# Turning the far half of the normalised input on VectorE, from an exchanged copy kept in DRAM, instead of on TensorE

## The chip, the cores and the metric

The kernel runs on one core of one Trainium2 chip. The metric is the device time of one execution in microseconds (us); of three runs of the kernel before, the median is 1872.5 us (1872.37 to 1872.6).

## The reference

One transformer block in float32, for 2048 positions of 1024 features and 32 heads of 32. The part that the change touches is the input of the first projections, the normalised x.

```python
qkv = layernorm(x) @ wqkv                       # 2048 x 1024 by 1024 x 3072
pq, pk = q_h @ w_phi_h, k_h @ w_phi_h           # per head, 32 x 32
phi = concat(softmax(p), softmax(-p))           # for q and for k
o = phi_q (phi_k^T v) / (phi_q . sum phi_k + 1e-6)
h = x + o @ wo
out = h + relu(layernorm(h) @ w1) @ w2          # 1024 -> 3584 -> 1024
```

## The kernel before, in words

Every large product is made of matmuls with 128 x 128 stationary and 128 x 512 moving values. Float32 precision is kept by splitting each operand into a high part (float32 rounded to the matmul's type) and a low part (what is left); `mm3` (lines 182 to 184) adds high by high, high by low and low by high, so three matmuls make one **step** of the work.

The first stretch of the program, the projections, has 96 **items** of eight steps: 768 steps, counted from 0. An item multiplies one tile of 128 positions of normalised x by 512 columns of weights, one step for each of eight blocks k of 128 features. Eight items in a row (eight tiles) share the same eight weight tiles and make a **group** of 64 steps. The order is: for the near half of the positions (tiles 0 to 7), four groups for keys and values, kv (steps 0 to 255), and two for queries, q (256 to 383); then the same for the far half, tiles 8 to 15 (steps 384 to 767).

The names that matter around the change:

- `Units` hands out weights. A raw weight tile comes by DMA from SyncE's queue (SP) into one of six `raw` buffers; ScalarE (ACT) makes the high part (line 125), and VectorE (DVE) or GpSimd (POOL) the low part (line 129) into one of ten `w` buffers. Eight of the ten belong to the group in work, so only two weights of the next group, k0 and k1, can be made early. The others, k2 to k7, are made in the few steps around a **group change** (steps 64, 128, 192, 256, 320, 384, 448 and so on), each as soon as the last item of the old group has released a buffer. On POOL stand the lows of k2, k4 and k6 for kv groups, and of k3, k4, k6 and k7 for the near q groups.
- A tile of x is loaded, `ln_stats` (DVE) and `ln_power` (POOL, three small instructions, lines 231 to 233) give its mean and scale, `ln_norm` (ACT, line 239) normalises it, and `ln_turn` turns it: eight 128 x 128 transposes by TensorE (PE, line 246) into two banks of PSUM, from which `split` writes high (ACT, line 178) and low part (DVE, line 179) into the tile's `xT`. For the far tiles the statistics are taken early (x is loaded, read and let go), the normalising and turning happen beside the second q group, one tile in eight steps from step 321, and x is loaded a second time for it.
- `kv_z` (POOL, lines 452 and 454) adds each item's features of the keys into `zacc`. `q_fourth` (POOL, line 544) multiplies two small tiles per q item.
- The two last matrices are multiplied by a scheme with seven products in place of eight, which needs sums of blocks of w1 and w2. `t_load` (SP, line 353) brings a piece b of 512 KB, `t_sum` (POOL, line 363) makes four sums of 128 x 256 in it, `t_store` (SP, line 366) puts it back in DRAM. The table `sums_at` sets the step of each of the 56 pieces, and `home` its buffers: two in `tsp`, two in `fp` while that pool lives (until step 256), later two in `fp_ln`, the pool of the normalised tiles `xn`.

Nothing is scheduled at run time. `when(step, f, ...)` and `do(item, k, f, ...)` put calls into a table, and the program is written out in that order; each engine then runs its own instructions strictly in order, waiting for data and buffers. An instruction that waits holds up all that stand behind it on its engine. This holds for SP's DMA issues as well.

## Time and profile before

| | us |
|---|---|
| median of 3 runs | 1872.5 |
| the profiled execution, by its own clock outside | 1870.48 |
| its span, from first to last instruction | 1868.7 |
| PE busy in the span | 1856.5 |
| DVE busy | 1063.8 |
| ACT busy | 770.5 |
| POOL busy | 979.0 |

The profile is of one execution. A line such as "start, length, engine, line of the program, operation, out<-in, shapes, count, [idle before <- who ended the wait]" is one instruction, or several equal ones in a row. The table of waits gives for each waiting engine and line the time in total, the times, and the longest. Durations of neighbouring instructions on an engine can overlap a little, since they are pipelined: the distance of the starts is the cost.

### The profile page before, as it was taken

The numbers are of one execution on the slowest core, as the hardware profiler recorded it, in microseconds if no ns is written. First come the engines' busy times: TensorE is split into PE (matmuls) and PEld (weight loads), VectorE is DVE, ScalarE is ACT, GpSimd is POOL, SyncE is SP. The second block draws the span as 40 slices with busy tenths as digits, with TensorE's granted clock in tenths as the row PEclk, the third lists the DMA queues.
The fourth block names the chain that finished last, engine by engine and source line by source line (L and its number), as shares of the span: only waits on it lengthen the run. The fifth ranks groups of instructions, "written<-read, shape, count | busy, mean of one in ns | idle before, by whom it ended". The sixth has DMA issues, their size and how long they took to land.

```text
span 1868.7 us, 28840 instructions
## 1 busy us (share of the span) xinstructions
PE 1856.5 (99%) x10064; PEld 1516.3 (81%) x10064; DVE 1063.8 (57%) x1655; ACT 770.5 (41%) x1379; POOL 979.0 (52%) x991
## 2 busy tenths in 40 slices
PE   9999999999999999999999999999999999999999
PEld 7777788888887777888888888888888888888887
DVE  7787678677689878575555653443433333343333
ACT  5322245233333333354455554444444444444442
POOL 4887745888947988343333222222344444444443
PEclk9999999999999999999999999999999999999999
DMA  7988798666575676887888975666677677777765
GB/s 229 286 294 288 231 289 270 190 203 202 178 227 181 223 243 203 280 278 232 247 262 259 324 249 184 193 201 205 225 223 215 216 218 239 238 215 217 216 216 177
DMA packets 333635, 433.04 MB, mean 232 GB/s; under 512 B 28720, under 2 KB 194608, under 8 KB 333488
## 3 DMA queue, kind: packets, MB, share of 16 engines
q1 hardware_dynamic: 299696, 414.41, 70.1%
q10 hardware_dynamic: 33792, 16.78, 3.2%
q8 instruction: 79, 1.29, 0.3%
q14 instruction: 68, 0.56, 0.1%
HBM read 293.21 MB, written 137.89 MB: 231 GB/s over the span
## 4 chain that ended last, share of the span: by engine, by line
PE 93%; DVE 3%; POOL 1%; issue 1%; ACT 0%; DMA 0%; SPq 0%; ACTq 0%; DVEq 0%; POOLq 0%
PE mm L182 24%; PE mm L183 24%; PE mm L184 24%; PE ac L182 4%; PE ac L184 4%; PE ac L183 4%; PE tp L184 2%; PE tp L183 2%; PE tp L182 2%; PE tp L246 1%; PE ac L465 1%; PE ac L650 1%; DVE qsm L534 0%; DVE qe L637 0%; POOL w L129 0%
## 5 line engine op out<-in xcount | busy, mean ns | idle before, releaser
L129 POOL TENSOR_TENSOR w<-raw,w 128x512 fp32r<-128x512 f32 x353 | 469.0, 1331 | 698.3 <-ACT w L125 663.2
L125 ACT ACTIVATE w<-raw 128x512 fp32r<-128x512 f32 x686 | 409.4, 626 | 508.8 <-PE mm L184 232.4
L129 DVE TENSOR_TENSOR w<-raw,w 128x512 fp32r<-128x512 f32 x333 | 271.0, 815 | 511.6 <-ACT w L125 507.6
L182 PE MATMUL mm<-w,xT 128*128 128x512 f32 x768 | 306.0, 398 | 0.0
L183 PE MATMUL mm<-w,xT 128*128 128x512 f32 x768 | 300.2, 391 | 0.4 <-POOL w L401 0.4
L184 PE MATMUL mm<-w,xT 128*128 128x512 f32 x768 | 299.6, 390 | 0.0
L182 PE MATMUL mm<-hT,w 128*128 128x512 f32 x672 | 261.5, 389 | 0.0
L183 PE MATMUL mm<-hT,w 128*128 128x512 f32 x672 | 261.5, 389 | 0.0
L184 PE MATMUL mm<-hT,w 128*128 128x512 f32 x672 | 261.5, 389 | 0.0
L182 PEld LDWEIGHTS mm<-w,xT 128*128 128x128 f32 x768 | 144.4, 188 | 35.2 <-issue 4.1
L184 PEld LDWEIGHTS mm<-w,xT 128*128 128x128 f32 x768 | 144.4, 188 | 30.9
L363 POOL TENSOR_TENSOR b<-b 128x256 f32<-128x256 f32 x176 | 143.6, 816 | 48.0 <-DMA b<-in_w_dram 38.6
L183 PEld LDWEIGHTS mm<-w,xT 128*128 128x128 f32 x768 | 144.6, 188 | 29.2 <-POOL w L401 1.0
L184 PE MATMUL mm<-w 128*128 128x512 f32 x392 | 152.6, 389 | 0.0
L182 PE MATMUL mm<-w 128*128 128x512 f32 x392 | 152.6, 389 | 0.0
L183 PE MATMUL mm<-w 128*128 128x512 f32 x392 | 152.6, 389 | 0.0
L182 PEld LDWEIGHTS mm<-hT,w 128*128 128x128 f32 x672 | 126.2, 188 | 26.4
L183 PEld LDWEIGHTS mm<-hT,w 128*128 128x128 f32 x672 | 126.2, 188 | 26.2
L184 PEld LDWEIGHTS mm<-hT,w 128*128 128x128 f32 x672 | 126.2, 188 | 26.0
L183 PEld LDWEIGHTS mm<-w 128*128 128x128 f32 x392 | 73.6, 188 | 15.3
L184 PEld LDWEIGHTS mm<-w 128*128 128x128 f32 x392 | 73.6, 188 | 15.2
L182 PEld LDWEIGHTS mm<-w 128*128 128x128 f32 x392 | 73.6, 188 | 15.3
(173 smaller groups left out, 3106.0 us busy)
## 6 DMA issues: line engine op xcount, KB each, us to landing
raw<-t SPq DMA_DIRECT2D x224, 256.0 KB, 3.9
raw<-ad SPq DMA_DIRECT2D x196, 256.0 KB, 3.0
raw<-in_w_dram SPq DMA_DIRECT2D x168, 256.0 KB, 3.1
ad<-c SPq DMA_DIRECT2D x112, 256.0 KB, 3.6
b<-in_w_dram SPq DMA_DIRECT2D x44, 512.0 KB, 5.8
t<-b SPq DMA_DIRECT2D x44, 512.0 KB, 5.0
ad<-s SPq DMA_DIRECT2D x84, 256.0 KB, 4.1
ed<-qe ACTq DMA_DIRECT2D x64, 256.0 KB, 4.1
```

The lines of the kernel that those rows point to most:

```text
L125: nc.scalar.activation(w[:, 0, :], raw[1], AF.Copy)
L129: eng.tensor_tensor(out=w[:, 1, :], in0=raw[1], in1=w[:, 0, :].bitcast(F32), op=ALU.subtract)
L182: pe.matmul(ps, a_hi, b_hi, start=first, stop=False, skip_group_check=more)
L183: pe.matmul(ps, a_hi, b_lo, start=False, stop=False, skip_group_check=more)
L184: pe.matmul(ps, a_lo, b_hi, start=False, stop=last, skip_group_check=more)
L246: pe.transpose(pt[:, k, :], xn[:, (4 * j + k) * P:(4 * j + k + 1) * P], ident)
L363: pool.tensor_tensor(out=tsum[*u, *out], in0=tsum[*u, *a], in1=tsum[*u, *b], op=ALU.subtract)
L465: pe.matmul(kv_ps[s][g][32 * i:32 * (i + 1), 0:64], vt[:, 32 * h:32 * (h + 1)], phi[:, 64 * h:64 * (h + 1)], start=first, stop=last)
L650: pe.matmul(banks[g][32 * c:32 * (c + 1), 256 * j:256 * (j + 1)], kvL[rows, 2 * q + h // 4, 32 * (h % 4):32 * (h % 4 + 1)], phT_of[u - 1 + ...
```

## The change

The far tiles are no longer turned by PE. Their early pass keeps its result: after `ln_power`, the new `far_norm` (ACT) normalises the tile and writes it with the blocks of 32 features in another order, and `far_keep` (SP) stores it in DRAM as `xm`, with 32-row blocks of positions and quarters of features exchanged. Later `far_back` (SP) loads that copy (four tiles at steps 250 to 265, the other four 32 steps before their turning), and `far_turn` (DVE) turns it in place by 32 x 32 blocks, which with the exchange makes the full transpose. `far_high` (ACT) and `far_low` (POOL, 128 x 1024) make the two parts of `xT`, reading the turned tile through `far_view`, in which neighbouring elements lie 256 apart. 

The early pass goes from one tile in 16 steps (from step 80) to one in 26. The turning goes from one tile in 8 steps (from 321) to one in 11 (from 330, so that the last four tiles are turned in the first items of the far half, at steps 374 to 417). In `sums_at` the two pieces at 332 and 342 are taken away and the ten from step 202 to 296 become twelve from step 198 to 293, seven to ten steps apart in place of nine to nineteen.

```diff
+    xm = {t: dram.tile([P, D], F32, name=f"xm{t}") for t in range(HT, NT)}
...
     def ln_load(key, parts):
-        xin[key] = xlp.tile([P, D], F32, name="xl") if key[0] == "x" and key[1] >= HT and key[1] % 4 > 1 else \
-            lnp.tile([P, D], F32, name="xin")
+        xin[key] = lnp.tile([P, D], F32, name="xin")
...
+    def far_norm(t):
+        sc, src = xst.pop(("s", t)), xin.pop(("s", t))
+        xin["m", t] = y = lnp.tile([P, D], F32, name="xin")
+        act.activation(y.rearrange("p (a c k) -> p c a k", a=4, c=NK), src.rearrange("p (c a k) -> p c a k", a=4, c=NK),
+                       AF.Identity, bias=sc[:, 1:2], scale=sc[:, 0:1])
+
+    def far_keep(t):
+        sp.dma_start(xm[t].rearrange("(a t) (g x) -> (t g) a x", a=4, g=4),
+                     xin.pop(("m", t)).rearrange("p (a x) -> p a x", a=4))
+
+    def far_back(t):
+        xnt["x", t] = y = xlp.tile([P, D], F32, name="xl") if t % 4 > 1 else fp_ln.tile([P, D], F32, name="xn")
+        sp.dma_start(y, xm[t])
+
+    def far_turn(t):
+        v.transpose(xnt["x", t], xnt["x", t])
+
+    def far_view(y):
+        return y.rearrange("p (g c t) -> p c t g", g=4, c=NK)
+
+    def far_high(t):
+        act.activation(xT[t][:, 0].rearrange("p c (t g) -> p c t g", g=4), far_view(xnt["x", t]), AF.Copy)
+
+    def far_low(t):
+        lo, hi = (xT[t][:, s].rearrange("p c (t g) -> p c t g", g=4) for s in (1, 0))
+        pool.tensor_tensor(out=lo, in0=far_view(xnt.pop(("x", t))), in1=f32(hi), op=ALU.subtract)
...
-            early = 80 + 16 * (t - HT)
+            early, late_ = 80 + 26 * (t - HT), 330 + 11 * (t - HT)
             when(early, ln_load, ("s", t), x_part(t))
-            when(early + 18, ln_stats, ("s", t))
-            when(early + 18, xin.pop, ("s", t))
-            when(early + 22, ln_power, ("s", t))
-            load_ = turn - 88 + 8 * (t - HT) if t < HT + 4 else turn - 36
-            stages = (load_, None, None, turn - 8, turn + 1, turn + 1)
+            when(early + 12, ln_stats, ("s", t))
+            when(early + 16, ln_power, ("s", t))
+            when(early + 20, far_norm, t)
+            when(early + 23, far_keep, t)
+            when(250 + 5 * (t - HT) if t < HT + 4 else late_ - 32, far_back, t)
+            do(n, 0, x_open, t)
+            for step, f in ((0, far_turn), (6, far_high), (10, far_low)):
+                when(late_ + step, f, t)
+            continue
...
-    sums_at = [30, 39, 47, 55] + [64 * i + k for i in (1, 2, 3) for k in sixth] + \
-        [266, 276, 286, 296, 332, 342, 352, 362, 372] + [64 * i + k for i in (6, 7, 8, 9) for k in sixth] + [650]
+    sums_at = [30, 39, 47, 55] + [64 * i + k for i in (1, 2) for k in sixth] + \
+        [198, 205, 212, 219, 226, 233, 243, 253, 263, 273, 283, 293, 352, 362, 372] + [64 * i + k for i in (6, 7, 8, 9) for k in sixth] + [650]
...
-        when(step - (7 if 256 < step < 400 else 15), t_load, w, p, j, home)
+        when(step - (7 if 240 < step < 400 else 15), t_load, w, p, j, home)
```

Three places of POOL's queue, each before and after the change. The line numbers of the changed kernel are higher by 27: 363 becomes 390 (sums), 454 becomes 481 (`kv_z`), 544 becomes 571 (`q_fourth`); 129 (lows of weights) and 231 to 233 (`ln_power`) keep theirs. In the names, w is a weight, raw its source, b or xn a piece of sums, zacc the sum over the keys' features, sc or scx the mean and scale of a tile of x, xT a turned tile.

The first place is the group change at step 128. Before, POOL's row from the `ln_power` at step 118 to the lows of k4 and k6:

```order
L231 TENSOR_SCALAR scx<-mv 128x1
L232 TENSOR_TENSOR scx<-scx,half 128x1
L233 TENSOR_SCALAR scx<-mv,scx 128x1
L363 TENSOR_TENSOR b<-b 128x256 x2
L129 TENSOR_TENSOR w<-raw,w 128x512
L363 TENSOR_TENSOR b<-b 128x256
L454 TENSOR_TENSOR zacc_361<-zacc_361,kphi 128x512
L363 TENSOR_TENSOR b<-b 128x256
L129 TENSOR_TENSOR w<-raw,w 128x512 x2
```

The same place on POOL in the changed kernel, where the first w is again k2 and the pair k4 and k6:

```order
L390 TENSOR_TENSOR b<-b 128x256 x2
L129 TENSOR_TENSOR w<-raw,w 128x512
L390 TENSOR_TENSOR b<-b 128x256
L231 TENSOR_SCALAR sc<-mv 128x1
L232 TENSOR_TENSOR sc<-sc,half 128x1
L233 TENSOR_SCALAR sc<-mv,sc 128x1
L481 TENSOR_TENSOR zacc_369<-zacc_369,kphi 128x512
L390 TENSOR_TENSOR b<-b 128x256
L129 TENSOR_TENSOR w<-raw,w 128x512 x2
```

The `ln_power` (now at step 122) has moved from ahead of the sums to a place behind k2 and ahead of k4 and k6.

The second place is the group change at step 256, the opening of the first q group. Before, POOL's lows are k3, and after one `kv_z` and one sum k4, k6 and k7 together:

```order
L363 TENSOR_TENSOR b<-b 128x256 x3
L129 TENSOR_TENSOR w<-raw,w 128x512
L454 TENSOR_TENSOR zacc_363<-zacc_363,kphi 128x512
L363 TENSOR_TENSOR b<-b 128x256
L129 TENSOR_TENSOR w<-raw,w 128x512 x3
L454 TENSOR_TENSOR zacc_363<-zacc_363,kphi 128x512
```

The same place on POOL in the changed kernel, from the four sums of the piece at step 243:

```order
L390 TENSOR_TENSOR b<-b 128x256 x4
L129 TENSOR_TENSOR w<-raw,w 128x512
L481 TENSOR_TENSOR zacc_371<-zacc_371,kphi 128x512
L129 TENSOR_TENSOR w<-raw,w 128x512
L231 TENSOR_SCALAR sc<-mv 128x1
L232 TENSOR_TENSOR sc<-sc,half 128x1
L233 TENSOR_SCALAR sc<-mv,sc 128x1
L129 TENSOR_TENSOR w<-raw,w 128x512
L390 TENSOR_TENSOR b<-b 128x256
L129 TENSOR_TENSOR w<-raw,w 128x512
L390 TENSOR_TENSOR b<-b 128x256 x3
L481 TENSOR_TENSOR zacc_371<-zacc_371,kphi 128x512
```

A whole piece (step 243) now ends just ahead of k3, an `ln_power` (step 252) stands between k4 and k6, and the first sum of the next piece (step 253) between k6 and k7.

The third place is the first group of the far half, steps 394 to 448, up to the row that is followed by the low of k2 for the group change at step 448. Before, from the second of its pieces:

```order
L363 TENSOR_TENSOR b<-b 128x256 x4
L454 TENSOR_TENSOR zacc_360<-zacc_360,kphi 128x512
L363 TENSOR_TENSOR xn<-xn 128x256 x4
L454 TENSOR_TENSOR zacc_360<-zacc_360,kphi 128x512
L363 TENSOR_TENSOR xn<-xn 128x256 x4
L454 TENSOR_TENSOR zacc_360<-zacc_360,kphi 128x512
L363 TENSOR_TENSOR b<-b 128x256 x4
L454 TENSOR_TENSOR zacc_360<-zacc_360,kphi 128x512
L363 TENSOR_TENSOR b<-b 128x256 x2
L129 TENSOR_TENSOR w<-raw,w 128x512
```

The same place on POOL in the changed kernel:

```order
L390 TENSOR_TENSOR b<-b 128x256 x3
L281 TENSOR_TENSOR xT<-xl,xT 128x1024
L390 TENSOR_TENSOR b<-b 128x256
L481 TENSOR_TENSOR zacc_368<-zacc_368,kphi 128x512
L390 TENSOR_TENSOR xn<-xn 128x256 x4
L281 TENSOR_TENSOR xT<-xl,xT 128x1024
L481 TENSOR_TENSOR zacc_368<-zacc_368,kphi 128x512
L390 TENSOR_TENSOR xn<-xn 128x256 x4
L481 TENSOR_TENSOR zacc_368<-zacc_368,kphi 128x512
L390 TENSOR_TENSOR b<-b 128x256 x4
L481 TENSOR_TENSOR zacc_368<-zacc_368,kphi 128x512
L390 TENSOR_TENSOR b<-b 128x256 x2
```

The low parts of tiles 14 and 15 (line 281) have come into this row; that of tile 13 stands one piece earlier, and that of tile 12 just behind the low of k6 for the group change at step 384.

4 lines of the change are left out of this document (2 added, 2 removed).

## The prediction, as it was put on record

> **What bounds the kernel now.** I read the page first, then the waits of PE, and then PE's own row of time where the far tiles are turned.
>
> ```profile
> span 1868.7 us, 28840 instructions
> PE 1856.5 (99%) x10064; PEld 1516.3 (81%) x10064; DVE 1063.8 (57%) x1655; ACT 770.5 (41%) x1379; POOL 979.0 (52%) x991
> PE 93%; DVE 3%; POOL 1%; issue 1%; ACT 0%; DMA 0%; SPq 0%; ACTq 0%; DVEq 0%; POOLq 0%
> ```
>
> PE works through 99% of the span, and the chain that ended last is PE for 93%. So the time falls by what PE no longer does, and rises by what PE has to wait that it doesn't wait now.
>
> ```profile
> PE ac L650 <- DVE qe L637: 2.8, 2, 2.4
> ```
>
> This is the first of five rows, the longest in total: no line of PE waits more than 2.8 us in the whole program, and none of the five lies in the stretch that changes. There is no wait to win there, only work.
>
> ```profile
> 268.78 0.39 PE L184 MATMUL mm<-w,xT 128*128 128x512 f32 x1
> 269.01 1.03 PE L246 MATMUL tp<-ident,xn 128*128 128x128 f32 x8
> 269.80 0.48 PE L182 MATMUL mm<-w,xT 128*128 128x512 f32 x1
> 270.12 0.40 PE L183 MATMUL mm<-w,xT 128*128 128x512 f32 x1
> ```
>
> A matmul comes every 0.227 us (0.68 us a step, 5.44 us an item). Between 269.01 and 270.12 stand eight transposes and one matmul: 1.11 - 0.23 = 0.88 us for the transposes.
>
> ```profile
> 269.17 0.87 PE tp L246 x8
> ...
> 313.61 0.87 PE tp L246 x8
> ```
>
> In the chain, the first and last of the eight far tiles lie 44.44 us apart, 6.35 us an item in place of 5.44: 0.91 us a tile.
>
> **The change part by part.** *PE's transposes.* 64 of 176 leave. Eight times 0.91 is **7.3 us less**, and this is the whole gain that the change can have.
>
> *What the turning costs elsewhere.*
>
> ```profile
> L637 DVE STREAM_TRANSPOSE qe<-qe 128x1024 f32<-128x1024 f32 x32 | 39.3, 1227 | 7.5 <-POOL qe L631 5.6 <-POOL qe L626 1.8
> L179 DVE TENSOR_TENSOR xT<-tp,xT 128x512 fp32r<-128x512 f32 x32 | 20.7, 679 | 11.1 <-ACT xT L178 11.1
> L631 POOL TENSOR_TENSOR qe<-qe,qden 128x1024 f32<-128x1024 f32 x26 | 50.3, 1935 | 3.1 <-DVE qden L621 3.0
> L129 POOL TENSOR_TENSOR w<-raw,w 128x512 fp32r<-128x512 f32 x353 | 469.0, 1331 | 698.3 <-ACT w L125 663.2 <-DMA ad<-s 12.1 <-DVE c L866 8.3
> L667 DVE TENSOR_TENSOR oT<-ac,oT 128x512 fp32r<-128x512 f32 x32 | 20.2, 673 | 3.3 <-ACT oT L657 3.3
> L781 DVE STREAM_TRANSPOSE y<-xin 128x1024 f32<-128x1024 f32 x4 | 8.2, 2040 | 1.2 <-ACT xin L796 1.2
> 262.00:311.00 49.00, 49.00 (x246) 41.12 (x245) 41.92 (x66) 28.05 (x38) 24.30 (x42) 1.00 0.90 276
> ```
>
> DVE gives up two differences of 0.68 us a tile (1.36) and gets one turn, for which the in-place turn of the same size is the row: 1.23. That is even. Beside the second q group DVE is busy 41.92 of 49 us, and there the items get 14% shorter, so its cover is thin: 41.92 over 7.7 items of 6.35 is 5.4 us of work for an item that will last 5.44. I cost it at nothing, because an item's bank is needed again only three items later; once DVE falls over 10 us behind, PE waits. ACT trades two copies of 512 for one of 1024 beside 28 of 49 us: nothing. A load, a store and a load in place of two loads are eight transfers of 512 KB more, on queues that wait for nothing of theirs: nothing by themselves.
>
> POOL gets `far_low`, **d** us each, eight times, and no row shows a POOL difference that reads elements 256 apart. Below, the shortest POOL row of that size (L631, one operand repeated) is 1.94. Contiguous, two lows of 512 take 2.66. Above, DVE pays 2.04 in place of 1.23 where its turn runs over spread elements (L781 against L637), a factor 1.66: 4.4 by that. The nearest row is the difference of the same kind, L129, so d = 2.66, with 1.94 and 4.4 kept.
>
> [...]
>
> *What gets in front of weights.* POOL matters to PE only at group changes, where it must make lows between the release of a buffer and the use. So each is a sum of its own.
>
> At step 128:
>
> ```profile
> 109.41 0.22 POOL L231 TENSOR_SCALAR scx<-mv 128x1 f32<-128x1 f32 x1 [2.91 <-DVE mv L224]
> ...
> 111.04 1.55 POOL L363 TENSOR_TENSOR b<-b 128x256 f32<-128x256 f32 x2
> 112.92 1.30 POOL L129 TENSOR_TENSOR w<-raw,w 128x512 fp32r<-128x512 f32 x1 [0.33 <-ACT w L125]
> ...
> 118.22 3.00 POOL L129 TENSOR_TENSOR w<-raw,w 128x512 fp32r<-128x512 f32 x2
> 120.75 0.39 PE L183 MATMUL mm<-w,xT 128*128 128x512 f32 x1
> ```
>
> The first of the pair at 118.22 is k4, done at 119.7; the last row is PE's first use of it (the item's fifth step). Slack 1.0. From 112.92 on POOL has no gap. The order puts an `ln_power` into that row, which now takes 109.41 to 111.04 = 1.63 in a gap. So PE waits 0.6; if the two sums of the row, 1.19 each beside DVE's work, shrink to the 0.73 that a sum takes undisturbed (the row at 321.66 below), nothing. I take **0.5**, range 0 to 0.9.
>
> At step 256:
>
> ```profile
> 184.64 1.29 POOL L129 TENSOR_TENSOR w<-raw,w 128x512 fp32r<-128x512 f32 x1 [2.88 <-ACT w L125]
> ...
> 212.96 1.52 POOL L129 TENSOR_TENSOR w<-raw,w 128x512 fp32r<-128x512 f32 x1 [4.74 <-ACT w L125]
> ...
> 215.68 1.19 POOL L363 TENSOR_TENSOR b<-b 128x256 f32<-128x256 f32 x1
> 216.84 4.24 POOL L129 TENSOR_TENSOR w<-raw,w 128x512 fp32r<-128x512 f32 x3
> 222.19 0.39 PE L183 MATMUL mm<-w,xT 128*128 128x512 f32 x1
> b<-in_w_dram SPq DMA_DIRECT2D x44, 512.0 KB, 5.8
> t<-b SPq DMA_DIRECT2D x44, 512.0 KB, 5.0
> ```
>
> The last of the three at 216.84 is k7, done at 221.08 and used at 222.19: slack 1.1. Two things are new. An `ln_power` (1.6) stands in the row; the sum there has only changed its place. And the whole piece of step 243 stands ahead of k3. When can it be done? Behind the weight that ends at 185.9 stand three pieces (four sums, 3.2 each), two `kv_z` (1.3 each) and an `ln_power`: 199.7 for the piece at step 226. That piece's buffer is what the piece at 243 needs: store 5.0, load 5.8, issue 0.5, its sums 3.2: 214.2. Now k3 starts at 212.96; it starts 1.2 later. PE waits 1.6 + 1.2 - 1.1 = 1.7. If the piece lands early, 0.5; I take **1.5**, range 0 to 3.
>
> At step 384:
>
> ```profile
> 302.76 3.19 POOL L363 TENSOR_TENSOR b<-b 128x256 f32<-128x256 f32 x4 [2.85 <-DMA b<-in_w_dram]
> ...
> 311.48 1.29 POOL L129 TENSOR_TENSOR w<-raw,w 128x512 fp32r<-128x512 f32 x1
> ...
> 312.99 0.39 PE L183 MATMUL mm<-w,xT 128*128 128x512 f32 x1
> ```
>
> A `far_low` goes between the sums. The items ahead are 0.91 shorter each, and the piece, which comes by its own load, is about 1.5 later against PE. So k2 starts at 302.76 + 1.5 + 3.19 + 2.66 = 310.1 in this clock and is done at 311.4, used at 312.99. k4 follows at 312.7 and k6 (the row at 311.48, now done at 312.77) at 314.6, used two and four steps after k2, 314.4 and 315.7. **Nothing**; with d = 4.4, 0.1 to 2. But k6 is 1.9 later than now.
>
> At step 448:
>
> ```profile
> 321.66 0.73 POOL L363 TENSOR_TENSOR b<-b 128x256 f32<-128x256 f32 x1 [1.19 <-DMA b<-in_w_dram]
> ...
> 345.19 1.30 POOL L454 TENSOR_TENSOR zacc<-zacc,kphi 128x512 f32<-128x512 f32 x1 [0.73 <-DVE kphi L446]
> 346.45 1.55 POOL L363 TENSOR_TENSOR b<-b 128x256 f32<-128x256 f32 x2
> 353.12 1.30 POOL L129 TENSOR_TENSOR w<-raw,w 128x512 fp32r<-128x512 f32 x1 [5.12 <-ACT w L125]
> ...
> 358.42 2.99 POOL L129 TENSOR_TENSOR w<-raw,w 128x512 fp32r<-128x512 f32 x2
> 360.94 0.39 PE L183 MATMUL mm<-w,xT 128*128 128x512 f32 x1
> 358.00:405.00 47.00, 47.00 (x323) 37.85 (x322) 31.76 (x64) 16.14 (x36) 40.96 (x41) 1.00 0.60 196
> ```
>
> Here is the largest term. From 321.66 to 348.0 POOL has work with one gap (0.7), then 5.1 us of rest before k2. Into this row come three `far_low` (tiles 13, 14, 15): 3 x 2.66 = 8.0. The row also starts about 1.9 later, because SP issues its first load only behind the raw weights that wait for k6; and PE reaches step 448 0.9 sooner, the transposes of step 386 being gone. So k2 starts 8.0 + 1.9 + 0.9 - 5.1 - 0.7 = 5.0 late. k4 (done 359.9, used 360.94) has 1.0 of slack: PE waits 4.0. The row from 353.12 to 359.9 takes 6.8; with the sums and `kv_z` in it at their undisturbed 0.73 and 1.29, since DVE's own work then no longer falls beside them, 5.4: PE waits 2.6. I take **3.0**, range 1 to 4, at this d, and four times what d exceeds 2.66 on top (the one ahead of k6 and the three). In the 47 us that follow POOL is busy 40.96 (the last row), so it is level again before step 512 and nothing is carried on.
>
> *Sum.* -7.3 + 0.5 + 1.5 + 0 + 3.0 = **-2.3 us**. The profiled execution was 1870.48: 1868.2. The median of the runs shown is 2.0 higher than that execution, so I carry the difference over to it: 1872.5 - 2.3 = **1870.2**.
>
> **The rivals.** *Nothing is late.* For it: POOL is only 24.30 of 49 us busy beside the second q group, and each of the three waits is a small difference of large numbers, with 0 in two of the ranges. Against: at 448 eight microseconds meet five of rest. It gives 1872.5 - 7.3 = 1865.2.
>
> *The spread read is slow.* One mechanism, one place: `far_low` in the first far group, at four microseconds of PE for each that d rises. From d = 3.2 the gain is gone, from d = 4.2 the kernel is slower by over 0.2%. At the upper bound 4.4 it is 4 x 1.74 = 7.0 more: 1877.2, and a late k4 or k6 at 384 could add 1 or 2. For it: L781 against L637. Against: where DVE reads spread elements from PSUM it pays nothing (L667 0.67, L179 0.68), and POOL takes twice DVE's time for the same difference as it is. [...]
>
> *SP is held up.* `far_keep` waits for ACT, which waits for `ln_power` on POOL, which is behind its sums; behind it on SP stand the loads of pieces and raw weights. `far_back` of tiles 12 to 15 waits for the `far_low` that lets go its buffer, and the load of the next piece stands just behind. Each microsecond that the piece of step 243 lands later costs one at step 256; held for the four sums of one more piece, 3.2: 1873.4. For it, the waits of SP's queue between 60 and 420 us:
>
> ```profile
> SPq L353 <- DMA t<-b: 23.9, 6, 5.2
> ```
>
> Loads of pieces already wait for stores of pieces, up to 5.2 us. Against: each `far_norm` stands four steps (2.7 us) behind its `ln_power`.
>
> That the change doesn't do what it says can be left out: PE's rows in the order lack the 64 transposes.
>
> **How the numbers follow.** Forecast 1870.2: chance 0.38, by itself 1867 to 1873. Nothing late: 0.25. Slow read: 0.25. SP held up: 0.12. A measurement of this kernel can tell about 0.2%, 3.75 us, from no change. Faster by more than that (under 1868.75): the 0.25 and 0.07 of the forecast's lower end, 0.32. Slower (over 1876.25): most of the slow read, some of the third, 0.24. Within: 0.44. The range goes from the full gain, 1865, to the slow read's upper bound, 1878.
>
> **What would show it.** PE's table of waits in the changed profile: rows of `mm L183` <- POOL `w L129` with the sizes above, two or three of them, none over 4 us. POOL's mean for line 281 decides between the forecast (under 3) and the slow read (over 3.2). The items beside the second q group should be 5.44 us apart. If PE waits for nothing at 256 and 448, the first rival is right; if PE waits for `xT` of line 281 or for banks of DVE, I have missed a chain altogether.

## The result, and the profile after

The changed kernel takes **1883.43 us** (median of six runs, 1882.78 to 1886.47) beside 1872.66 for the kernel before on the same chip: a ratio of 1.0061 (95% interval 1.0051 to 1.0071). It is slower by 10.8 us. The forecast was 1870.2, with a range from 1865 to 1878.

The page of the changed kernel, the same three lines as before:

```profile
span 1884.6 us, 28715 instructions
PE 1859.1 (99%) x10000; PEld 1515.6 (80%) x10000; DVE 1071.7 (57%) x1647; ACT 778.5 (41%) x1371; POOL 1001.0 (53%) x999
PE 85%; DVE 4%; POOL 4%; DMA 4%; issue 2%; ACT 1%; ACTq 0%; SPq 0%; POOLq 0%; DVEq 0%
```

PE lost 64 instructions and is busy longer all the same; its part of the chain fell from 93 to 85%. PE's waits in the changed kernel (us in total, times, longest):

```profile
PE mm L183 <- POOL w L129: 7.1, 7, 2.6
PE ac L492 <- DVE kphi L473: 3.6, 1, 3.6
PE tp L246 <- ACT xn L239: 2.8, 1, 2.8
PE mm L183 <- DVE w L129: 2.6, 2, 1.6
```

Of the first, second and fourth row there was nothing before. The third is at the start of the program. This profiled execution (1886.47) is the longest of its six: by step 8 it is 3.7 us late already (2.2 in one other profile of this study, under 0.8 in the rest), and that much is left out below.

How late each item begins against the same item before tells where the time went. The eight items that lost their transposes (41 to 48) are each 0.9 us shorter, 7.2 together. The losses stand at six places:

| begins to be late at step | us lost | predicted |
|---|---|---|
| 128 | 0.6 | 0.5 |
| 256 | 1.1 | 1.5 |
| 320 | 2.9 | no term |
| 384 | 1.9 | 0 |
| 424 | 5.4 (3.8 waiting, 1.6 of clock) | no term |
| 448 | 6.3 | 3.0 |

Together 18.2; less 7.2, that is 11.0, beside 10.8 measured. What lies behind step 768 is left out: the profiles of this study are 0.4 to 2.4 us longer there than that of before (one is level), also that of a kernel whose program is the same there (the second experiment, 2.4). So it seems to be the execution profiled before that was short there.

**At 128 and 256: `ln_power` stands in POOL's row.** At 256 it stands there together with the piece of step 243, as the prediction had it. POOL waits for the load of that piece and then makes k3:

```profile
214.76 3.19 POOL L390 TENSOR_TENSOR b<-b 128x256 f32<-128x256 f32 x4 [4.02 <-DMA b<-in_w_dram]
217.91 1.30 POOL L129 TENSOR_TENSOR w<-raw,w 128x512 fp32r<-128x512 f32 x1
```

Before, k3 began at 212.96. PE comes 4.3 us later here (3.7 of them from the start of the program), so k3 is 0.6 later against PE.

**At 320: ACT waits in order.** The early pass, ACT's row of the changed kernel (start, length, then as in the sections above; `far_norm` is L259, line 125 makes the highs of weights):

```profile
237.04 1.06 ACT L552 ACTIVATE qe<-qe 128x1024 f32<-128x1024 f32 x1 [5.19 <-DVE qe L548]
...
252.25 1.24 ACT L259 ACTIVATE xin<-xin,sc 128x1024 f32<-128x1024 f32 x1 [14.14 <-POOL sc L233]
...
267.23 3.23 ACT L125 ACTIVATE w<-raw 128x512 fp32r<-128x512 f32 x6 [1.51 <-PE mm L184]
```

The same six highs before:

```profile
257.84 3.24 ACT L125 ACTIVATE w<-raw 128x512 fp32r<-128x512 f32 x6 [1.16 <-PE mm L184]
```

ACT stood 14 us at the `far_norm` of the last tile. POOL's row shows why its scale came so late (L390 are sums, L231 begins `ln_power`), and DVE's that the x of that tile had come late too:

```profile
247.69 3.19 POOL L390 TENSOR_TENSOR b<-b 128x256 f32<-128x256 f32 x4 [3.88 <-DMA b<-in_w_dram]
250.97 0.22 POOL L231 TENSOR_SCALAR sc<-mv 128x1 f32<-128x1 f32 x1
```
```profile
243.67 1.29 DVE L222 BATCH_NORM_STATS2 st<-xin 128x6 f32<-128x512 f32 x2 [6.66 <-DMA xin<-in_x_dram]
```

`ln_power` stood behind sums that waited for their loads. The exponentials of the first q group queued behind ACT, and the highs for step 320 began 9.4 us later than before where PE was 5.4 us later.

**At 384: SP waits in order.** SP's waits between 290 and 420 us, and POOL's row up to the pair k2, k4 of step 384:

```profile
SPq L268 <- POOL xT L281: 13.4, 3, 7.1
```
```profile
308.08 0.73 POOL L390 TENSOR_TENSOR b<-b 128x256 f32<-128x256 f32 x1 [3.57 <-DMA b<-in_w_dram]
308.77 2.97 POOL L281 TENSOR_TENSOR xT<-xl,xT 128x1024 fp32r<-128x1024 f32 x1
...
314.90 2.96 POOL L129 TENSOR_TENSOR w<-raw,w 128x512 fp32r<-128x512 f32 x2
```

SP stood at `far_back` (L268) until a `far_low` (L281) let go its buffer; the load of the piece at step 372 came behind, POOL idled 3.57 us for it, and k2 was ready only at 316.62, when PE had stood waiting for it for 1.47 us.

**At 424: ACT is late, and DVE's `kphi` stands while POOL's `far_low` runs.** DVE's row, POOL's and PE's, and then all that `kphi` took in the program:

```profile
326.95 0.42 DVE L457 TENSOR_REDUCE kmx<-mm 128x8 f32<-128x256 f32 x1 [6.42 <-ACT vt L454]
...
332.48 3.32 DVE L473 TENSOR_TENSOR kphi<-ke,ksm 128x512 f32<-128x512 f32 x1
...
344.41 1.72 DVE L473 TENSOR_TENSOR kphi<-ke,ksm 128x512 f32<-128x512 f32 x1
```
```profile
332.29 2.95 POOL L281 TENSOR_TENSOR xT<-xn,xT 128x1024 fp32r<-128x1024 f32 x1
...
342.73 2.85 POOL L281 TENSOR_TENSOR xT<-xl,xT 128x1024 fp32r<-128x1024 f32 x1
```
```profile
346.27 0.43 PE L492 MATMUL ac<-kphi,vt 128*32 128x64 f32 x16 [3.64 <-DVE kphi L473]
```

```profile
L473 DVE TENSOR_TENSOR kphi<-ke,ksm x64: 691/852/3318, 30.5 to 522.2; 128x512 f32<-128x512 f32 x64
```

The last row gives the least, the median and the most that one `kphi` takes, in ns: 0.69 us where nothing is in its way. Both times it began while `far_low` ran, and it ended 0.56 and 0.55 us after `far_low` had ended: it did not run slower, it stood. The profiles of this study have 31 such `kphi`, in 14 kernels; each ends 0.54 to 0.56 us after its `far_low`, however early it began. What stands behind `kphi` on DVE stands too, ACT's exponential waits for that (3.40 us at 337.15, 4.68 at 342.74), and the next `vt` behind it. DVE had begun the group late already, by the 6.42 us of waiting for ACT.

ACT in turn was late with the first `vt` of the group, and what stands ahead of it on ACT are two pairs of its own DMA issues, of copies of `ed`, and a `far_high` of 2.06 us:

```profile
315.66 4.15 ACTq L556 DMA_DIRECT2D ed<-qe  x2
321.01 2.91 ACTq L556 DMA_DIRECT2D ed<-qe  x2
326.55 0.38 ACT L454 ACTIVATE vt<-mm 128x256 f32<-128x256 f32 x1
```

The last pair and the first `vt` before:

```profile
317.47 0.95 ACTq L529 DMA_DIRECT2D ed<-qe  x2
319.00 0.37 ACT L427 ACTIVATE vt<-mm 128x256 f32<-128x256 f32 x1
```

This `vt` comes 5.7 us behind the end of its item on PE, before 1.2. In the kernels of the table below that lose 3.5 us or more at 424 it comes 5.7 to 7.9 behind (4.1 in the one with a piece at 342), in the other changed kernels 3.2 to 4.6. One issue takes 0.4 us (the median of this line's 64); ACT stands 3.4 and 2.1 us between the two of a pair. What holds it there the trace doesn't name, and no experiment tests it.

**At 448: POOL's row is full.** POOL between 350 and 378 us, and the clock behind PE's waits (stretch, length, busy time of PE, PEld, DVE, ACT and POOL, granted clock, DMA share, GB/s):

```profile
347.70:351.10 3.40, 3.40 (x10) 2.63 (x9) 2.82 (x7) 0.75 (x2) 3.17 (x5) 0.50 0.86 213
375.00:378.40 3.40, 3.40 (x10) 2.63 (x9) 0.00 (x0) 0.23 (x1) 3.40 (x4) 0.50 0.92 275
```
```profile
350.00:378.00 28.00, 23.94 (x139) 18.64 (x139) 16.35 (x32) 7.66 (x14) 27.37 (x25) 0.93 0.50 149
```
```profile
369.66 0.50 PE L183 MATMUL mm<-w,xT 128*128 128x512 f32 x1 [1.45 <-POOL w L129]
...
373.95 0.50 PE L183 MATMUL mm<-w,xT 128*128 128x512 f32 x1 [2.62 <-POOL w L129]
```

POOL is busy 27.37 of 28 us. PE waits 4.1 us for k2 and k4, and then works at half clock for 3.4 us, as it does behind the wait at 346.27; each such stretch costs about 1.7, half of its 3.4. The row was also late as a whole: its first piece was begun at 331.59, 18.1 us behind PE's step 384, and before 10.3 behind (321.66), for POOL stood 5.55 us for the load of that piece.

### The profile page after: what moved, and what is told of

The parts are those of the page before. It is cut to its first block, busy times and chain, and to the rows that moved or that the text cites. A ratio compares the mean times of both kernels' runs of the same rounds, so it can differ in the third digit from the quotient of the medians.

```text
span 1884.6 us, 28715 instructions
## 1 busy us (share of the span) xinstructions
PE 1859.1 (99%) x10000; PEld 1515.6 (80%) x10000; DVE 1071.7 (57%) x1647; ACT 778.5 (41%) x1371; POOL 1001.0 (53%) x999
## 3 DMA queue, kind: packets, MB, share of 16 engines
q8 instruction: 78, 1.28, 0.3%
## 4 chain that ended last, share of the span: by engine, by line
PE 85%; DVE 4%; POOL 4%; DMA 4%; issue 2%; ACT 1%; ACTq 0%; SPq 0%; POOLq 0%; DVEq 0%
PE mm L182 21%; PE mm L183 21%; PE mm L184 21%; PE ac L182 4%; PE ac L183 4%; PE ac L184 4%; PE tp L183 2%; PE tp L184 2%; PE tp L182 2%; DMA b<-in_w_dram 1%; POOL b L390 1%; POOL w L129 1%; DMA t<-b 1%; PE ac L492 1%; PE tp L246 1%
## 5 line engine op out<-in xcount | busy, mean ns | idle before, releaser
L390 POOL TENSOR_TENSOR b<-b 128x256 f32<-128x256 f32 x176 | 145.6, 828 | 42.2 <-DMA b<-in_w_dram 33.5
L481 POOL TENSOR_TENSOR zacc<-zacc,kphi 128x512 f32<-128x512 f32 x60 | 81.5, 1358 | 11.6 <-DVE kphi L473 11.6
L182 PEld LDWEIGHTS mm<-w 128*128 128x128 f32 x392 | 73.6, 188 | 15.3
L183 PEld LDWEIGHTS mm<-w 128*128 128x128 f32 x392 | 73.6, 188 | 15.3
```

Of the source, the lines that this page charges most:

```text
L182: pe.matmul(ps, a_hi, b_hi, start=first, stop=False, skip_group_check=more)
L183: pe.matmul(ps, a_hi, b_lo, start=False, stop=False, skip_group_check=more)
L390: pool.tensor_tensor(out=tsum[*u, *out], in0=tsum[*u, *a], in1=tsum[*u, *b], op=ALU.subtract)
L481: pool.tensor_tensor(out=zacc[s], in0=zacc[s], in1=phi_of[key], op=ALU.add)
```

## The experiments

Theory: four in-order queues (POOL, ACT, SP, DVE) are late at six places, each for a reason of its own. Rivals: the packed sums carry one lateness through; the added transfers do it; the spread read does it, as the prediction's second rival had it. All runs but two (the four stores, below) in one table: us lost at each place, with the 0.9 of a transpose taken out, from one profile each; then the median in us and the ratio to before. The profiles differ among themselves: six kernels that have the same program up to step 320 (the change, `far_low` on DVE, load back later, contiguous, three sums away, other order of elements) lose 1.2 to 3.1 there, and the three at the foot, also alike up to there, 1.4, 1.4 and 0.

| kernel | 128 | 256 | 320 | 384 | 424 | 448 | 640 | median | ratio, 95% |
|---|---|---|---|---|---|---|---|---|---|
| the change | 0.6 | 1.1 | 2.9 | 1.9 | 5.4 | 6.3 | 0 | 1883.4 | 1.0051 to 1.0071 |
| old sums | 0.6 | 0.5 | 0.7 | 6.8 | 1.8 | 6.2 | 0 | 1883.1 | 1.0038 to 1.0068 |
| sums alone (on before) | 0 | 0 | 0 | 0 | 0 | 0 | 0 | 1873.2 | 0.9994 to 1.0012 |
| `far_low` on DVE | 0.6 | 1.9 | 1.2 | 3.9 | 7.5 | 0 | 0 | 1880.2 | 1.0025 to 1.0055 |
| last norm later | 0.6 | 1.1 | 1.6 | 1.6 | 5.2 | 6.3 | 0 | 1880.5 | 1.0028 to 1.0057 |
| load back later | 0.6 | 1.4 | 2.8 | 0.1 | 5.5 | 6.3 | 0 | 1882.0 | 1.0037 to 1.0070 |
| contiguous | 0.6 | 1.1 | 2.4 | 0 | 0 | 8.8 | 0 | 1879.9 | 1.0024 to 1.0054 |
| three sums away | 0.6 | 1.2 | 1.8 | 1.5 | 5.9 | 0 | 3.9 | 1881.0 | 1.0033 to 1.0063 |
| three edits | 0.6 | 1.3 | 0.6 | 0 | 1.1 | 1.6 | 2.2 | 1875.3 | 1.0006 to 1.0024 |
| other order of elements | 0.6 | 1.3 | 3.1 | 1.3 | 6.4 | 3.6 | 0 | 1881.7 | 1.0035 to 1.0065 |
| pass of 22 steps | 0 | 0.1 | 1.6 | 2.1 | 3.5 | 8.5 | 0 | 1880.2 | 1.0027 to 1.0055 |
| rows of x reordered | 0.6 | 1.3 | 2.6 | 0 | 0.5 | 5.5 | 0 | 1877.1 | 1.0016 to 1.0037 |
| all, a piece at 342 | 0 | 0.9 | 1.4 | 2.9 | 3.6 | 0 | 0 | 1872.3 | 0.9989 to 1.0007 |
| all, four pieces | 0 | 0.9 | 1.4 | 0 | 0 | 0 | 0 (0.4 at 576) | **1867.5** | 0.9959 to 0.9981 |
| all, three pieces | 0 | 1.1 | 0 | 0 | 1.1 | 0 | 0 (0.8 at 576) | 1869.8 | 0.9977 to 0.9995 |

**The sums: old places in the changed kernel, new places in the kernel before.** Only `sums_at` and the lead of its loads are exchanged.

```diff
-    sums_at = [30, 39, 47, 55] + [64 * i + k for i in (1, 2) for k in sixth] + \
-        [198, 205, 212, 219, 226, 233, 243, 253, 263, 273, 283, 293, 352, 362, 372] + [64 * i + k for i in (6, 7, 8, 9) for k in sixth] + [650]
+    sums_at = [30, 39, 47, 55] + [64 * i + k for i in (1, 2, 3) for k in sixth] + \
+        [266, 276, 286, 296, 332, 342, 352, 362, 372] + [64 * i + k for i in (6, 7, 8, 9) for k in sixth] + [650]
...
```

> The changed kernel with the old places of the weight sums. The profile of the changed kernel puts PE's losses at step 128 (0.6 us), 256 (1.1), 320 (2.9), 384 (1.9), 424 (3.8 and 1.6 of clock) and 448 (6.0). Theory A, that POOL is late at the group changes because `far_low` and `ln_power` stand in its row, and that ACT waits in order behind `ln_power`: the losses at 384, 424 and 448 stay within 1 us, those at 256 and 320 shrink together by 1 to 3, so 1880 to 1882.5. Rival B, that the packed sums made POOL late and everything behind is carried on from there: all but about 2 us of the losses go, 1871 or less. Rival C, that the traffic of the stored copy is the cause: no change, 1883.

> The kernel before with the new places of the sums alone. Theory A: between 0 and 1.5 us at step 256 and nothing at 320, so 1872.5 to 1874. Rival B: most of what the change lost beyond the transposes, 1880 or more.

The packed sums cost nothing by themselves: 1873.2, as theory A said. With the old ones 256 and 320 lose 2.8 less, as theory A said, but 384 loses 4.9 more, which it had excluded: the pieces at 332 and 342 fall among the `far_low`. So the median, 1883.1, misses theory A's range and stands where rival C had it, because gains and losses cancel; the places tell them apart. Packing the sums earlier was needed; it is not the cause.

**`far_low` on DVE.**

```diff
-        pool.tensor_tensor(out=lo, in0=far_view(xnt.pop(("x", t))), in1=f32(hi), op=ALU.subtract)
+        v.tensor_tensor(out=lo, in0=far_view(xnt.pop(("x", t))), in1=f32(hi), op=ALU.subtract)
```

> The changed kernel with `far_low` on DVE in place of POOL. Theory A: POOL has 8 x 2.96 us less between steps 340 and 430, so the losses at 384, 424 and 448 go (up to 13 us, clock included), those before stay; DVE's own row there gets 8 differences of 1.1 to 2 us and could give back 0 to 4: 1871 to 1875. Rival C (the copy's traffic, or DVE's turn): less than 3 us gained, over 1880.

448 loses nothing, so POOL's row is what was late there. But 384 and 424 lose more (PE waits for `kphi`, 5.0): DVE's eight differences take 1.98 and 2.22 us on average, at and above the top of what I had assumed, in a row that has no room for them. Half a hit: 1880.2 where 1871 to 1875 was expected. The time alone lies where rival C had it (over 1880); that 448 goes wholly does not fit C.

```profile
L281 DVE TENSOR_TENSOR xT<-xl,xT 128x1024 fp32r<-128x1024 f32 x4 | 8.9, 2220 | 0.0
L281 DVE TENSOR_TENSOR xT<-xn,xT 128x1024 fp32r<-128x1024 f32 x4 | 7.9, 1976 | 0.0
```

**The last tile's normalizing later.**

```diff
+            rest = 14 if t == NT - 1 else 0
-            when(early + 20, far_norm, t)
-            when(early + 23, far_keep, t)
+            when(early + 20 + rest, far_norm, t)
+            when(early + 23 + rest, far_keep, t)
```

> The changed kernel with the normalizing and the store of tile 15 14 steps later, so that ACT no longer reaches it 14 us before POOL has its scale. Theory A: ACT's wait for `sc` falls from 14 us to under 5, the weights at step 320 come in time, its 2.9 us shrink to under 0.7, nothing else moves: about 1880.5. Rival D, that the second q group was late by itself (its exponentials and DVE's part): 320 keeps over 2 us, 1883.

ACT's row of this kernel; the wait of 14.14 is now 1.12, and the highs of step 320 begin 6.25 us sooner, where PE comes 3.0 sooner:

```profile
251.78 1.25 ACT L259 ACTIVATE xin<-xin,sc 128x1024 f32<-128x1024 f32 x1 [1.12 <-DMA b<-in_w_dram]
...
260.98 3.24 ACT L125 ACTIVATE w<-raw 128x512 fp32r<-128x512 f32 x6 [1.03 <-PE mm L184]
```

320 loses 1.6 in place of 2.9, and 0.6 in the later kernel that has the same edit, where the six kernels without it lose 1.2 to 3.1: ACT's wait has a part, about as large as what the profiles differ by. That the time is the one expected (1880.5) is partly luck, since this place gave only 1.3 of the 2.9 us. What stays is another queue's. PE waits 1.28 us there for a low of DVE's, and DVE had stood ahead of it for `q_fourth` on POOL (`smq`), which itself stood behind a piece that waited 3.00 us for its load; no experiment tests this.

```profile
261.48 1.22 DVE L561 TENSOR_REDUCE qsm<-qe 128x32 f32<-128x1024 f32 x1 [2.62 <-POOL smq L571]
...
265.33 1.58 DVE L129 TENSOR_TENSOR w<-raw,w 128x512 fp32r<-128x512 f32 x1
```

**`far_back` ten steps later.**

```diff
-            when(250 + 5 * (t - HT) if t < HT + 4 else late_ - 32, far_back, t)
+            when(250 + 5 * (t - HT) if t < HT + 4 else late_ - 22, far_back, t)
```

> The changed kernel with `far_back` of tiles 12 to 15 issued 22 steps ahead of its turn in place of 32. In the changed kernel SP stood at three of these loads for up to 7.1 us until `far_low` let go the buffer, and the load of the sums of step 372 stood behind. Theory E, that this wait of SP is what makes POOL late at step 384: the piece lands 2 to 3 us sooner, POOL's 3.6 us of idle time ahead of it goes, k2 of step 384 is in time (0.1 or less lost in place of 1.9), and step 424 loses 0 to 2 us in place of 3.8 and its 1.6 of clock; step 448 keeps 4 or more: 1877 to 1880. Rival F, that POOL's own load is what is late: less than 1 us gained, 1882.5 or more.

384 is in time, as theory E said: POOL no longer idles ahead of it (its row of this kernel; the pair k2, k4, which began at 314.90 in the changed kernel, is 5.9 us sooner, PE 3.1):

```profile
303.78 2.96 POOL L281 TENSOR_TENSOR xT<-xl,xT 128x1024 fp32r<-128x1024 f32 x1
306.71 2.37 POOL L390 TENSOR_TENSOR b<-b 128x256 f32<-128x256 f32 x3
309.04 3.08 POOL L129 TENSOR_TENSOR w<-raw,w 128x512 fp32r<-128x512 f32 x2
```

424 keeps 5.5, where E had 0 to 2. So SP's wait explains 384 and not 424, and the time, 1882.0, missed the expectation.

**Contiguous reads.** The tile that comes out is another one than the reference's.

```diff
-        return y.rearrange("p (g c t) -> p c t g", g=4, c=NK)
+        return y.rearrange("p (c t g) -> p c t g", g=4, c=NK)
```

> The changed kernel with `far_high` and `far_low` reading the stored rows in the order in which they lie, and writing the same tile (the tile that it makes is another one than the reference's). What the spread read costs by itself: `far_low` 2.4 to 2.7 us in place of 2.96, `far_high` about 1.05 in place of 2.10. Theory A: lateness at 384 to 448 falls by 4 x 0.3 to 0.6, so 1 to 3 us less, 1880 to 1882.5. If the spread read is the cause (the rival of the prediction), more than 6 us go, under 1877.5. In both cases a DVE difference that starts while `far_low` runs should still end about 0.56 us behind it.

`far_low` takes 2.40, `far_high` 1.06. 384 and 424 lose nothing; 448 loses 8.8, more than before this edit, since PE comes 8 us sooner to a POOL row that is not as much shorter. The total, 1879.9, is just under theory A's range, and A had not expected 424 to go wholly.

**Three pieces of sums away from between 384 and 448.**

```diff
-        [198, 205, 212, 219, 226, 233, 243, 253, 263, 273, 283, 293, 352, 362, 372] + [64 * i + k for i in (6, 7, 8, 9) for k in sixth] + [650]
+        [198, 205, 212, 219, 226, 233, 243, 253, 263, 273, 283, 293, 352, 362, 372] + [64 * i + k for i in (6, 7, 8, 9) for k in (range(6, 64, 9) if i > 6 else sixth[3:])] + [650]
...
-        half_on = sums_at.index(64 * 6 + 10)
+        half_on = sums_at.index(64 * 6 + 37)
```

> The changed kernel with the weight sums of steps 394, 403 and 412 taken to steps behind 448 (seven a group in place of six). Theory A, that at step 448 POOL's row is too full: some 9 to 13 us of POOL's work leave it, the loss of 6.0 falls to under 1 and the clock does not fall there; 424 loses as much as before or less (its loss is of DVE and ACT): 1876 to 1878.5. Rival E, that the late loads on SP are the cause throughout: 448 still loses over 3, 1881 or more.

448 loses nothing, a hit. But the same POOL work now makes 640 late by 3.9: seven pieces a group are one too many ahead of a group change with more lows. The total gained 2.5 in place of 5 to 7.

**Three edits together:** the last norm later, the load back later, three sums away.

> The three edits together: the last normalizing 14 steps later, `far_back` 10 steps later, three sums taken from between 384 and 448. If the losses have the three separate causes named so far they add up: left are 0.6 at step 128, 1.1 at 256, 1.6 at 320, 0 to 1.5 at 424, 0 to 1 at 448 and 1.1 in the attention, against 7.2 gained: 1870 to 1873. If one loss stands in for another (a time that is only handed on), 1875 or more.

The median, 1875.3, lies just inside the second branch. By place most of it adds up: 320, 384 and 424 fall together to 1.7, from 10.2. 424 loses 1.1 although none of the three alone had changed it: it seems to need more than one queue to be late. 640 loses 2.2, which I had left out of the sum, and 448 loses 1.6.

**Another order of the same elements.** The stored row is read as it lies, and `xT` written 16 bytes apart.

```diff
-        return y.rearrange("p (g c t) -> p c t g", g=4, c=NK)
+        return y.rearrange("p (g c t) -> p c g t", g=4, c=NK)
...
-        act.activation(xT[t][:, 0].rearrange("p c (t g) -> p c t g", g=4), far_view(xnt["x", t]), AF.Copy)
+        act.activation(xT[t][:, 0].rearrange("p c (t g) -> p c g t", g=4), far_view(xnt["x", t]), AF.Copy)
...
-        lo, hi = (xT[t][:, s].rearrange("p c (t g) -> p c t g", g=4) for s in (1, 0))
+        lo, hi = (xT[t][:, s].rearrange("p c (t g) -> p c g t", g=4) for s in (1, 0))
```

> The changed kernel with `far_high` and `far_low` going through the same elements in another order: the stored row is read as it lies (runs of 32), and the elements of xT are written 16 bytes apart. The result is the reference's. If the price is that of reading elements 1 KB apart, `far_high` falls from 2.08 to about 1.05 us and `far_low` from 2.95 to about 2.4, as in the contiguous kernel, and 424 loses nothing: 1878 to 1881. If any order but the contiguous one costs, both stay and so does the time, 1883.

`far_high` 2.02 and `far_low` 2.93: nothing won in either, and the time, 1881.7, can't be told from that of the change (the intervals overlap). Turning the loop over does not help; one side stays spread.

**The first pass every 22 steps.**

```diff
-            early, late_ = 80 + 26 * (t - HT), 330 + 11 * (t - HT)
+            early, late_ = 74 + 22 * (t - HT), 330 + 11 * (t - HT)
```

> The changed kernel with the first pass over the far tiles every 22 steps from step 74 on (in place of every 26 from 80), so that no `ln_power` is given to POOL within 12 steps ahead of a group change and the last normalizing is at step 248 in place of 282. Theory A: 0 lost at step 128 (0.6 now), 0 to 1 at 256 (1.1 now; the piece of step 243 still stands ahead of k3), under 1.6 at 320 (2.9 now; 1.6 was left with the last normalizing alone moved), the rest as it is: 1878.5 to 1880.5. If the losses at 128 and 256 come from the sums or from the traffic, they stay, and only 320 changes.

128 and 256 lose 0 and 0.1: what they lost was the `ln_power` in POOL's row and not the traffic, which is the same. The piece of step 243 still stands ahead of k3 and by itself costs no more than that 0.1 here; in the three kernels with all edits, below, its load comes later. 448 loses 8.5 (10.2 us of half clock behind its waits in this profile), so 2.2 of the 4.8 won ahead are given back. The time, 1880.2, is in the range expected.

**Runs of 32 with four stores, alone and with all edits.** Each of the four stores takes one quarter of the features, so that the tokens land as 32 g + t; `far_high` and `far_low` go through the elements as in the next experiment.

```diff
+        y = xin.pop(("m", t))
+        for a in range(4):
+            sp.dma_start(xm[t][32 * a:32 * (a + 1), :].rearrange("t (g x) -> g t x", g=4), y[:, 256 * a:256 * (a + 1)])
```

> The changed kernel with the tokens in another order in the stored copy (32 g + t in place of 4 t + g; the store is then four issues of 128 KB), so that `far_high` and `far_low` read and write runs of 32 elements. The result is the reference's. If the step between elements is what costs, and not the shape, `far_high` takes 1.0 to 1.2 us and `far_low` 2.4 to 2.5, as in the contiguous kernel; then 384 and 424 lose nothing, and 448 more than now (7 to 9, the time that PE wins ahead of it being handed on to it), 1878.5 to 1881. If runs of 32 cost as spread elements do, 1883.

> All edits that took a loss away, together: runs of 32, the first pass every 22 steps from 74 on, `far_back` 22 steps ahead, and the three sums of steps 394 to 412 taken behind 448, none of them within 11 steps ahead of step 640. By the runs so far: 7.2 gained; lost 0 at 128, 0.1 at 256, 0.5 to 1.5 at 320, 0 at 384, 0 to 1 at 424, 0 to 2.5 at 448, 0 to 2.2 at 640, 1.1 in the attention: 1867 to 1872, beside 1872.5 of the kernel before. If time taken from one place only turns up at the next, 1874 or more.

Both miss far: 1901.9 and 1893.0 (ratios 1.0135 to 1.0169 and 1.0088 to 1.0118). The losses begin at step 184 and are 18 us by step 320 in the first. SP's issues of the stores (ns: least, median, most), and DVE's row:

```profile
L265 SPq DMA_DIRECT2D xm<-xin x32: 504/644/2732, 97.9 to 269.8; - x32
```
```profile
182.31 1.29 DVE L222 BATCH_NORM_STATS2 st<-xin 128x6 f32<-128x512 f32 x2 [7.30 <-DMA xin<-in_x_dram]
```

24 more issues of 0.64 us are 15 us more of SP in 170, the loads of x came late, and DVE stood at the statistics with the items' own work behind it. That the time of the issues is the reason is argued from these rows. The next kernel, with one store and the same runs of 32, does not have these losses.

**Runs of 32 with one store.** The rows of x are loaded in the other order instead.

```diff
-            when(early, ln_load, ("s", t), x_part(t))
+            when(early, ln_load, ("s", t), [x[t * P:(t + 1) * P, :].rearrange("(g t) d -> t g d", g=4)])
-        return y.rearrange("p (g c t) -> p c t g", g=4, c=NK)
+        return y.rearrange("p (g c t) -> p c g t", g=4, c=NK)
...
-        act.activation(xT[t][:, 0].rearrange("p c (t g) -> p c t g", g=4), far_view(xnt["x", t]), AF.Copy)
+        act.activation(xT[t][:, 0].rearrange("p c (g t) -> p c g t", g=4), far_view(xnt["x", t]), AF.Copy)
...
-        lo, hi = (xT[t][:, s].rearrange("p c (t g) -> p c t g", g=4) for s in (1, 0))
+        lo, hi = (xT[t][:, s].rearrange("p c (g t) -> p c g t", g=4) for s in (1, 0))
```

> The changed kernel with the rows of x loaded in another order (row 32 g + t to partition 4 t + g), so that the store stays one issue and `far_high` and `far_low` read and write runs of 32 elements. The result is the reference's. If the step between elements is what costs: `far_high` 1.0 to 1.2 us, `far_low` 2.4 to 2.5; steps 128, 256 and 320 lose what they lose in the changed kernel, 384 and 424 nothing, 448 7 to 9 (handed on): 1878 to 1881. If runs of 32 cost as spread elements do, 1883.

The groups of this kernel (busy us, mean ns of one):

```profile
L281 POOL TENSOR_TENSOR xT<-xn,xT 128x1024 fp32r<-128x1024 f32 x4 | 9.6, 2404 | 1.9 <-ACT xT L277 1.9
L281 POOL TENSOR_TENSOR xT<-xl,xT 128x1024 fp32r<-128x1024 f32 x4 | 9.6, 2400 | 2.2 <-ACT xT L277 2.2
L277 ACT ACTIVATE xT<-xl 128x1024 fp32r<-128x1024 f32 x4 | 4.2, 1057 | 8.6 <-DMA ed<-qe 5.2 <-DVE xl L271 3.4
L277 ACT ACTIVATE xT<-xn 128x1024 fp32r<-128x1024 f32 x4 | 4.2, 1054 | 2.7 <-DVE xn L271 1.6 <-PE mm L184 1.1
```

The durations are those of the contiguous kernel, and 384 and 424 lose 0 and 0.5. 6.4 us are won, the most of any single edit and more than the 2 to 5 expected: 448 lost 5.5 and did not rise. That is also over the 6 us that the contiguous experiment had set as the sign of the spread read; there 448 had taken back what 384 and 424 gave.

**All edits together, with the sums in three arrangements.** Reordered rows, pass of 22, load back later, and:

| kernel | pieces from step 293 to 447 | in the three groups from 448 on |
|---|---|---|
| all, a piece at 342 | 293, 342, 352, 362, 372, 421, 430, 439 | 7, 7 and 6, then 650 |
| all, four pieces | 293, 352, 362, 372, 412, 421, 430, 439 | 7, 7 and 6, then 650 |
| all, three pieces | 293, 352, 362, 372, 421, 430, 439 | 8, 7 and 6, then 650 |

> Together: these runs of 32, the first pass every 22 steps from 74 on, `far_back` 22 steps ahead, the three sums of steps 394 to 412 taken elsewhere (one to step 342, two to behind 448; six pieces in the group ahead of step 640, as before). If the losses add up: 7.2 gained; lost 0 at 128, 0.1 at 256, 0.6 to 1.6 at 320, 0 at 384, 0 to 0.5 at 424, 0 to 2 at 448, 0 at 640, 1.1 in the attention: 1867 to 1870.5, faster than the kernel before by 0.1 to 0.3%. If the time is handed on, 1873 or more.

> As j2, but with four pieces of sums between 384 and 448 in place of three, and none at step 342. If the piece at 342 made POOL late at 384 in j2: nothing lost at 384, 0 to 0.6 at 424, 0.5 to 3 at 448 (6.0 with six pieces, 0 with three), 1.5 at 320, 0.1 to 0.9 at 256: 1868 to 1871. If 384 and 424 lose as in j2, the piece was not the reason, and 1873 or more.

> As k1, with three pieces between 384 and 448 and eight between 448 and 512. Nothing lost at 384 and 448, 0 to 0.6 at 424; at step 512 POOL has 3.2 us more than before per added piece against some 6 us of rest in the group: 0 to 2 lost there; 1868 to 1871.

The first, 1872.3, met neither of its two branches; the second, 1867.5, came out just under its range; the third, 1869.8, lies inside, though 424 lost 1.1 where 0.6 was the most expected. The intervals of the last two overlap.

One piece among the `far_low`, at step 342 in place of 412, costs 6.5 us at 384 and 424 in these profiles (4.8 in the medians). Without it the time is **1867.5**, 0.30% under the kernel before (0.19 to 0.41%), and 15.9 under the change. Nothing is left for the six places but 2.3 us, so the traffic of the stored copy, which is still there, costs no more than that. 0.9 of it is at 256 again, although no `ln_power` stands among the weights: POOL's row of this kernel has the piece of step 243 later than the kernel with the pass of 22 steps, where POOL waited 2.61 us and k3 began at 214.08.

```profile
210.25 1.06 POOL L390 TENSOR_TENSOR b<-b 128x256 f32<-128x256 f32 x1 [3.63 <-DMA b<-in_w_dram]
215.04 1.64 POOL L129 TENSOR_TENSOR w<-raw,w 128x512 fp32r<-128x512 f32 x1
```

PE's waits in the kernel with four pieces:

```profile
PE ac L677 <- DVE qe L664: 2.9, 2, 2.4
PE tp L246 <- ACT xn L239: 2.2, 1, 2.2
PE mm L183 <- DVE w L129: 2.1, 2, 1.0
PE tp L1274 <- POOL ones L1270: 1.6, 1, 1.6
PE mm L183 <- POOL wf L129: 1.5, 1, 1.5
PE mm L183 <- POOL w L129: 0.6, 1, 0.6
```

## Why the prediction was wrong

The forecast was wrong because waits that I put at nothing cost 10.2 us: at 424 ("That is even", for DVE), at 320 ("nothing", for ACT) and at 384 ("about 1.5 later", for a load). The terms:

- **The gain** (-7.3): 7.2. Right.
- **Steps 128 and 256** (0.5 and 1.5): 0.6 and 1.1, right, and by the mechanism named: with `ln_power` out of the row they are 0 and 0.1. At 256 the piece of step 243 made k3 0.6 later where I had 1.2; with `ln_power`'s 1.6 and the slack of 1.1 that gives the 1.1 measured. The kernels with all edits, which lose 0.9 to 1.1 there while the piece's load comes late, show that the piece has a part.
- **d**: 2.95 where I took 2.66, below the point 3.2 from which the forecast's sum would have lost the gain. The same difference on contiguous elements takes 2.40, so the step costs 23%. The second rival falls as I priced it, at 448: d was not slow enough. But the spread read, its cause, is the largest that a single edit took away. Without the spread elements, and with the result kept, 6.4 us are won (rows of x reordered), at 384 and 424. It bears there by two ways that I had not priced, ACT's copy (2.08 us, I had set two copies of 512 equal to one of 1024) and the standing of DVE while `far_low` runs.
- **Step 448** (3.0, and four times the excess of d, 1.2: 4.2): PE's waits are 1.45 + 2.62 = 4.1. The mechanism was right: with three pieces away nothing is lost. That the size agrees is luck. The row began 7.9 us later against PE's step 384 than before, where I had 1.9, and PE came to step 448 7.3 later than I had it (1.9 and 5.4, lost at 384 and 424); the two nearly cancel. Where 424 loses nothing, the contiguous kernel loses 8.8 and the reordered rows 5.5 at a d of 2.40, for which my sum has 2.0. The 1.7 of half clock behind the waits was missing.
- **Step 384** (0): 1.9. The failed step is "the piece, which comes by its own load, is about 1.5 later". It was later by SP's standing at `far_back`. I had named that wait, in the third rival, and priced it only at step 256. Shown by the experiment that issues `far_back` later; the kernels with a shorter `far_low`, for which SP waits, lose nothing there either.
- **Step 320** (no term): 2.9. The failed step is "ACT trades two copies of 512 for one of 1024 beside 28 of 49 us: nothing". I looked at the far turning alone; the early pass also gives ACT an instruction that waits for POOL, 14.14 us long, with the exponentials and the weights of step 320 behind it. "Each `far_norm` stands four steps (2.7 us) behind its `ln_power`" counted steps of the program, where the queue of POOL was over 10 us late. Moving the last one took 1.3 of the 2.9 away in one kernel and 2.3 in another, where profiles of the same program differ by up to 1.9. The rest is by the rows DVE's wait for `q_fourth` on POOL, which is not tested.
- **Step 424** (no term): 5.4. The failed step is "That is even", for DVE: even in busy time, but not in when it can run. The threshold that I set, that PE waits once DVE is 10 us behind, agrees: the `kphi` that PE waited for ended 14.4 us after its item, against 4.5 before. "Nothing", for ACT, fails here too: its first `vt` was 4.5 us later against its item than before, and DVE waited for it.

The third rival came nearest (a wait on POOL handed through `far_norm` to ACT, `far_back` on SP), at the wrong places and at 3.2 us, where 320, 384 and 424 lost 10.2. The common error: each edit was costed by its engine's spare time, and only POOL was followed instruction by instruction through its row. Left open: which of ACT's late `vt` (and the stand at its own DMA issues ahead of it), DVE's standing and the late raw weights makes how much of 424. It goes or nearly goes where the spread elements are away, and falls to 1.1 where three other edits come together.

## What to carry to other kernels

When work goes from the engine that bounds the kernel to in-order engines with spare time, ask for each added instruction what it will wait for and what stands behind it; half-idle engines lost 18 us here for a gain of 7. Put an instruction that needs another engine's result, or a load that needs a buffer, well behind the time when these are ready in the real queue, and take other work out of the rows that end at a deadline; then the same change is worth 5 us. Test moves together as well as one by one: 424 stayed with each of three edits alone and fell with all three, and time won at one deadline was given back at the next.

## What the runs showed of the hardware

- In the changed kernel, after a wait of 3.64 us, and after two of 1.45 and 2.62 within 5, PE's clock is granted at 0.50 for 3.4 us; in the kernel with the pass of 22 steps 10.2 us of half clock stand behind the waits at 448. PE was not idle all the time ahead of these stretches: in the 3.41 us ahead of the first (344.29 to 347.70) it was busy for 1.43, in those ahead of the second (371.59 to 375.00) for 1.05. Cut the 18 profiles, from 60 us on, into windows of 3.41 us on whose edges the stretches begin. Of the windows at full clock, 41 are followed by half clock, and PE stood 1.76 us or more in each of them; 9473 are not, and it stood at most 1.74 in any of them. In the profiles of the kernel before and of the change alone it stood 1.89 us or more in the six that are followed by half clock, and at most 1.71 in the other 1053. So here a little over half of 3.41 us of waiting was enough. It makes the 4.1 us of waits at 448 cost 5.8.
- ACT's copy of 1024 float32 a partition takes 1.06 us where it reads and writes runs of 32 elements (rows of x reordered), and 2.0 to 2.1 where one side is spread over elements 1 KB (the change) or 16 bytes apart (other order of elements); POOL's difference takes 2.40 in the first, and 2.95 and 2.93 in the other two.
- DVE's `kphi` that begins while POOL's `far_low` runs stands until that has ended (31 times, each ending 0.54 to 0.56 us after it), and up to 3.32 us in the changed kernel, 3.38 in that with the old sums, passed for 0.69 us of work.
